# Blocks 0 and 1 of a two-network kernel run as one pair of half blocks

## The chip, the cores and the metric

The kernel runs on one core of a Trainium2 chip. Five engines matter: PE multiplies matrices, DVE (vector) and ACT (scalar) do elementwise work, POOL (GpSimd) does a few integer additions here, and SP issues nearly all transfers between HBM and the core's memory. The metric is the time of one execution in device microseconds, and less is better.

## The reference

Packed attention runs first: 32 packed queries p of each batch and head attend over k and v, and the 576 queries q then attend over the 32 packed results, which serve as keys and as values. The output is reordered to 4608 rows of 512 and goes through two networks, one with ELU and one that multiplies two products. The four large weights come as float64.

```python
def _attn_ref(q, k, v, p):                 # 8 batches, 8 heads, 576 x 64
    def sm_attn(qq, kk, vv):
        s = scale * np.matmul(qq, kk.transpose(0, 1, 3, 2))
        s = s - np.max(s, axis=-1, keepdims=True)
        a = np.exp(s)
        a = a / (np.sum(a, axis=-1, keepdims=True) + 1e-09)
        return np.matmul(a, vv)
    p_packed = sm_attn(p, k, v)            # 32 rows per head
    return sm_attn(q, p_packed, p_packed)
...
    h = x @ w_in                           # 4608x512 @ 512x2048
    g = np.where(h > 0.0, h, alpha * (np.exp(np.minimum(h, 0.0)) - 1.0))
    x = g @ w_out                          # 2048x512
...
    return (x @ w_a) * (x @ w_b) @ w_out2  # 512x1536, 1536x512
```

## The kernel before

A product in f32 is made of three matmuls: each factor is split in a high part, which ACT copies and rounds, and a low part, which DVE subtracts. So nearly every result that PE needs next passes ACT and then DVE.

**The first network** works on the batches as blocks. A block has two halves h of 288 rows and 16 slices f of the hidden width. One pair (h, f) is a step: `l1` (six matmuls, L453) multiplies the attention result `a2` of this half with packed weights `wr`; `act1` makes the ELU, with two passes on ACT (L461, L462), `gf` on DVE (L465), and the split `gr` with its high part on ACT (L467) and its low part on DVE (L469); two steps later `l2` (twelve matmuls, L475) adds gr times `wout` to four accumulators. The accumulators of a half go out through `x2_out`.

Attention is folded into the weights: `wp` multiplies 512 columns of w_in by the packed result of a batch, and `wps` splits that into one slot of a ring (`ring_r`, five slots of two tiles, L83). Four such chunks c serve the slices f = 4c to 4c+3 of both halves. The probabilities of q over the packed keys are made by `s2`, `s2t` (a transpose, L338), `sm2a` (row maximum L343, subtraction L344), `sm2b`, `sm2c` (L357, L358) and `sm2d`, which leaves them as a tile `a2` (L363, L365) for each half h and each r, four tiles in all. Ahead of that lie, for each batch, the transposes of k and q (`qkT`), `s1`, `sm1`, `aT`, `pp`, `pps` and `ppT`.

**Block 0** runs f 0 to 7 of both halves, then f 8 to 15 of both. The sums of the first part (part 1) are stored to HBM as `x2p`, and part 2 loads them and adds them on DVE (L490). Blocks 1 to 7 run all 16 slices of one half and then of the other, and need no partial sums.

**The weights of the first network** come in 32 pieces of 512 KB, 16 of w_in (`i0_0` to `i3_3`; i`c`_`j` is the j-th row block of chunk c) and 16 of w_out (`o0` to `o15`). A piece is loaded into one of five slots (tag wst) and converted from float64: two passes on ACT (L133, L134), two and one on DVE (L137, L138, L141), an integer addition on POOL (L144), and for w_out also a cast on ACT (L148) and a subtraction on DVE (L149).

**What sets the order.** Attention, conversions and loads are items with times in half steps; `run_until` emits what is due between the instructions of act1, and an item whose needs are missing waits with the rest of its chain. Up to the end of block 0 a scheduler then orders the instructions of each engine anew by its own estimate, and it may pull conversions far ahead. From block 1 on (`manual_schedule`) the order of the program is kept on PE, DVE and ACT. Each engine works its list in order, so a wait holds all that stands behind it. SP's list holds all loads and stores.

Of the kernel before, what the change touches and what calls it, by code (L numbers as in the profile page):

```python
# [20 lines left out]
P = 128  # L21
# [4 lines left out]
def program(tc, q, k, v, p, w_in, w_out, w_a, w_b, w_out2, out):  # L26
# [25 lines left out]
    RING = NCH + 1  # L52
# [8 lines left out]
    with ctx:  # L61
# [29 lines left out]
        x2p = [dram.tile([P, NDM, HS], F32, name=f"x2p{h}") for h in range(2)]  # L91
# [290 lines left out]
        def attention(b, tokens=False):  # L382

            u = []

            def add(at_half, fn, *a, takes=None, frees=None):
                u.append((at_half, lambda: fn(b, *a), takes, frees))

            def at_times(k, load_q, pt, s1s, sm1, q, sm1bs, at, at5, p, ppt, s2s, wps_):
# [92 lines left out]

        def x2_out(b, h, acc, part):

            for d0 in range(0, NDM, 2):
                t = stage.tile([P, 2, HS], F32, tag="wst", name=f"x2s{b}_{h}_{d0}_{part}")
                if part == 2:
                    nc.sync.dma_start(t, x2p[h][:, d0:d0 + 2, :])
                    for i in range(2):
                        nc.vector.tensor_tensor(t[:, i, :], acc[d0 + i][:, :HS], t[:, i, :], op=ALU.add)  # L490
                else:
                    nc.scalar.copy(t[:, 0, :], acc[d0][:, :HS])
                    nc.vector.tensor_copy(t[:, 1, :], acc[d0 + 1][:, :HS])
                nc.sync.dma_start((x2p[h] if part == 1 else x2d[b][h])[:, d0:d0 + 2, :], t)
# [84 lines left out]
        load_v(0)  # L579
        for t, fn, takes, frees in attention(0, tokens=True):  # L580
            if t > 64:
                t += 16
            elif 39 < t < 50:
                t += 27
# [342 lines left out]
```

## Time and profile before

| | us |
|---|---|
| median of three runs (1646.26 to 1648.41) | 1646.31 |
| the profiled run | 1646.58 |
| its span in the trace | 1644.8 |
| PE busy | 1569.8 |
| DVE busy | 1025.1 |
| ACT busy | 717.0 |
| POOL busy | 168.8 |

The span is what the trace covers, and 1.8 us of the profiled run lie around it. Busy shares of the whole span hide stages that differ: PE's 95% is made of a start in which it often waits and of a long rest in which it hardly does. So the rows further down are read by stretch. In them a wait names the instruction that ended it last.

### The profile page before, as it was taken

The page shows a single profiled execution, that of the slowest core. Times are in us where ns is not written, and L with a number is a line of the kernel's source. Part 1 is how long each engine was busy: PE and PEld are TensorE (multiplying, and loading weights), DVE is VectorE, ACT ScalarE, POOL GpSimd, SP SyncE. Part 2 cuts the span into 40 slices and gives each one's busy share as a digit, 9 for nine tenths or more (in the row PEclk, how much of TensorE's full clock was granted, in tenths as well). Part 3 has the DMA queues.
Part 4 walks back from the last instruction along what each step waited for, and adds up shares of the span by engine and source line. Part 5 has one row for each costly group of instructions (what it writes and reads, how often), then busy time and mean ns, then how long its engine had stood idle before and what let it go on. Part 6 is the DMA issues. An engine that isn't in the chain of part 4 may idle for free.

```text
span 1644.8 us, 27465 instructions
## 1 busy us (share of the span) xinstructions
PE 1569.8 (95%) x10824; PEld 1438.4 (87%) x10824; DVE 1025.1 (62%) x2054; ACT 717.0 (44%) x1579; POOL 168.8 (10%) x122
## 2 busy tenths in 40 slices
PE   5488999999999999999889999999999999999999
PEld 3376998989898999999788899989989989998997
DVE  6988676777777676755588735634545453563452
ACT  6675666666666666665433312312222221231211
POOL 3321010000000100011364100000000000000000
PEclk7599999999999999999999999999999999999999
DMA  8755334525262624114366745535445554552541
GB/s 253 179 162 129 105 102 103 131 53 142 76 158 69 154 80 110 47 66 144 117 229 233 268 148 185 221 136 207 180 166 188 213 201 147 184 208 107 211 180 39
DMA packets 214785, 247.95 MB, mean 151 GB/s; under 512 B 150144, under 2 KB 180864, under 8 KB 205440
## 3 DMA queue, kind: packets, MB, share of 16 engines
q1 hardware_dynamic: 214656, 246.19, 46.3%
q8 instruction: 85, 1.39, 0.3%
q14 instruction: 44, 0.36, 0.1%
HBM read 194.64 MB, written 51.51 MB: 150 GB/s over the span
## 4 chain that ended last, share of the span: by engine, by line
PE 79%; DVE 6%; issue 4%; ACT 3%; DMA 3%; POOL 3%; SPq 2%; DVEq 0%; POOLq 0%; ACTq 0%
PE x2a L475 21%; PE o L846 17%; PE B L802 12%; PE h L453 10%; PE C L802 8%; PE A L802 8%; POOL e L708 2%; SPq L164 1%; POOL wo L791 1%; DMA wst_i<-in_moe_w_in_dram 1%; DVE gr L469 1%; DVE gf L465 1%; PE pp L301 1%; ACT gr L467 0%; DVE wr L83 0%
## 5 line engine op out<-in xcount | busy, mean ns | idle before, releaser
L475 PE MATMUL x2a<-gr,wout 128*128 128x288 f32 x3072 | 466.2, 300 | 10.3 <-DVE gr L469 6.4
L475 PEld LDWEIGHTS x2a<-gr,wout 128*128 128x128 f32 x3072 | 424.1, 190 | 51.6 <-issue 12.3
L846 PE MATMUL o<-wo,c 128*128 128x512 f32 x1296 | 309.2, 393 | 0.0
L846 PEld LDWEIGHTS o<-wo,c 128*128 128x128 f32 x1296 | 243.7, 189 | 48.2
L802 PE MATMUL B<-s,e 128*128 128x384 f32 x1296 | 262.8, 337 | 11.1 <-DVE u L827 5.3
L453 PE MATMUL h<-a,wr 128*128 128x288 f32 x1536 | 251.2, 299 | 16.9 <-DVE gf L465 8.6
L453 PEld LDWEIGHTS h<-a,wr 128*128 128x128 f32 x1536 | 220.8, 191 | 26.4 <-DVE gf L465 12.9
L802 PEld LDWEIGHTS B<-s,e 128*128 128x128 f32 x1296 | 228.2, 189 | 15.2 <-DVE u L827 7.8
L802 PE MATMUL A<-s,e 128*128 128x384 f32 x864 | 174.7, 336 | 1.0 <-ACT p L825 1.0
L802 PE MATMUL C<-s,e 128*128 128x384 f32 x864 | 173.9, 335 | 0.0
L465 DVE SCALAR_TENSOR_TENSOR gf<-ge,h 128x288 f32<-128x288 f32 x256 | 113.7, 445 | 85.8 <-ACT ge L462 83.1
L467 ACT CAST gr<-gf 128x288 fp32r<-128x288 f32 x256 | 110.4, 432 | 129.8 <-DVE gf L465 128.7
L802 PEld LDWEIGHTS A<-s,e 128*128 128x128 f32 x864 | 153.8, 188 | 7.2 <-ACT p L825 1.3
L469 DVE TENSOR_TENSOR gr<-gf,gr 128x288 fp32r<-128x288 f32 x256 | 131.5, 514 | 34.4 <-ACT gr L467 32.3
L802 PEld LDWEIGHTS C<-s,e 128*128 128x128 f32 x864 | 152.8, 189 | 0.0
L82 ACT CAST c<-u 128x384 fp32r<-128x384 f32 x72 | 36.8, 512 | 230.3 <-DVE u L835 230.3
L461 ACT ACTIVATE ge<-h 128x288 f32<-128x288 f32 x256 | 104.5, 409 | 74.0 <-PE h L453 73.3
L832 DVE TENSOR_TENSOR v<-p,B 128x384 f32<-128x384 f32 x72 | 39.8, 552 | 143.3 <-PE B L802 143.2
L462 ACT ACTIVATE ge<-ge 128x288 f32<-128x288 f32 x256 | 113.8, 445 | 7.6
L827 DVE TENSOR_TENSOR u<-p,B 128x384 f32<-128x384 f32 x72 | 39.7, 552 | 105.1 <-PE B L802 105.1
L825 ACT COPY p<-A 128x384 f32<-128x384 f32 x72 | 34.7, 482 | 120.2 <-PE A L802 120.1
L829 ACT COPY p<-C 128x384 f32<-128x384 f32 x72 | 34.7, 482 | 102.2 <-PE C L802 102.2
(342 smaller groups left out, 1449.1 us busy)
## 6 DMA issues: line engine op xcount, KB each, us to landing
e<-ed SPq DMA_DIRECT2D x60, 1792.0 KB, 7.1
ed<-e SPq DMA_DIRECT2D x12, 1792.0 KB, 6.4
x2d<-x2s SPq DMA_DIRECT2D x32, 288.0 KB, 2.4
out_dram<-osb SPq DMA_DIRECT2D x36, 256.0 KB, 2.0
v<-in_v_dram SPq DMA_DIRECT2D x8, 1024.0 KB, 7.8
wst_i<-in_moe_w_in_dram SPq DMA_DIRECT2D x16, 512.0 KB, 5.4
wst_o<-in_moe_w_out_dram SPq DMA_DIRECT2D x16, 512.0 KB, 4.5
kst<-in_k_dram SPq DMA_DIRECT2D x112, 72.0 KB, 2.5
```

The costliest lines, as they stand in the source:

```text
L82: nc.scalar.copy(hi, src)
L453: nc.tensor.matmul(t[:, :HS], w[:, wi, o * P:(o + 1) * P], x[:, xi, :], start=(n == 0), stop=(n == 5))
L461: nc.scalar.activation(e, t[:, :HS], AF.Relu, scale=-1.0)
L462: nc.scalar.activation(e, e, AF.Exp, scale=-1.0)
L465: nc.vector.scalar_tensor_tensor(g, e, -1.0, t[:, :HS], op0=ALU.add, op1=ALU.max)
L467: nc.scalar.copy(gr[:, 0, :], g)
L469: nc.vector.tensor_tensor(gr[:, 1, :], g, gr[:, 0, :].bitcast(F32), op=ALU.subtract)
L475: nc.tensor.matmul(acc[d][:, :HS], wout_r[f][:, wi, d * P:(d + 1) * P], gr[:, xi, :], start=(first and n == 0), stop=(last and n == 2),)
L802: nc.tensor.matmul(bank[:, :HT], es[f][:, E_OF[i], wi, k * P:(k + 1) * P], ss[i][:, xi, k, :], start=(first and n == 0), stop=(n == 5), sk ...
L827: nc.vector.tensor_tensor(u, p1, pB, op=ALU.add)
L832: nc.vector.tensor_tensor(v, p1, pB, op=ALU.add)
L846: nc.tensor.matmul(acc, cr[:, xi, t * P:(t + 1) * P], wo[f][:, wi, :], start=(f == 0 and n == 0), stop=(f == NF2 - 1 and n == 2),)
```

## The change

Batches 0 and 1 run as one: part 1 is f 0 to 7 of batch 0 (both halves) and of batch 1 (both halves), part 2 is f 8 to 15 of the same four. So 32 steps run on the first eight slices and 32 on the last eight, and block 1 too stores partial sums and adds them. All eight `a2` tiles of the pair are kept. The ring has four slots: batch 0 uses slots 0 and 1, batch 1 slots 2 and 3, each twice, and from batch 2 on chunk c has slot c. The load of `x2p` is issued four steps before its adds. The first load of v stands behind the first three pieces of w_in on SP. The attention times of batches 0 and 1 are new, those of batches 2 to 7 shift a little, and o0 and o1 are converted ahead of the pieces of chunk 1. The scheduler still orders the first 32 steps; from part 2 on the program's order is kept. The new line numbers are L460 for l1, L472 for gf, L474 and L476 for gr, L482 for l2, L507 for the copy into x2s and L508 for its store.

```diff
-    RING = NCH + 1
+    RING = NCH
...
-        x2p = [dram.tile([P, NDM, HS], F32, name=f"x2p{h}") for h in range(2)]
+        x2p = [[dram.tile([P, NDM, HS], F32, name=f"x2p{b}_{h}") for h in range(2)] for b in range(2)]
...
-            a2 = m1.tile([P, 2, HS], F32R, tag="a2", name=f"a2_{b}_{h}_{r}", bufs=4)
+            a2 = m1.tile([P, 2, HS], F32R, tag="a2", name=f"a2_{b}_{h}_{r}", bufs=8)
...
-            slot = (b * NCH + c) % RING
+            slot = c if b > 1 else 2 * b + c % 2
...
-                at_times((-17, -14, -2, -1), (-13, 0), 0, (4, 6), (8, 9), (10, 11, 13, 14), 12, 14, 16, (18, 20, 21), 22, (
+                at_times((-17, -14, -4, -3), (-13, -2), -4, (4, 6), (8, 9), (10, 11, 13, 14), 12, 14, 16, (18, 20, 21), 22, (
...
-                ), (48, 52, 56, 60))
+                ), 70, (48, 52, 57, 62))
...
+        def x2_load(b, h):
+            for d0 in range(0, NDM, 2):
+                x2s[d0] = stage.tile([P, 2, HS], F32, tag="wst", name=f"x2s{b}_{h}_{d0}_2")
+                nc.sync.dma_start(x2s[d0], x2p[b][h][:, d0:d0 + 2, :])
...
-        load_v(0)
...
+        put(HEAD + 8.25, load_v, 0)
...
-        order = [("i", 0, j) for j in range(NJ)]
...
+        order = [("i", 0, j) for j in range(NJ)] + [("o", f, 0) for f in range(2)]
+        order += [("i", 1, j) for j in range(NJ)] + [("o", f, 0) for f in range(2, NF // 2)]
+        order += [("i", c, j) for c in (2, 3) for j in range(NJ)] + [("o", f, 0) for f in range(NF // 2, NF)]
...
-                t = 12 + 2.5 * (n - 16)
+                t = 8 + 2.6 * (n - 16)
...
+        def m1_steps(t0, bs, fs, part=0):
+
+            for n, (b, h, f) in enumerate([(b, h, f) for b in bs for h in range(2) for f in fs]):
+                first, last = f == fs[0], f == fs[-1]
...
+                if part == 2 and f == fs[-4]:
+                    x2_load(b, h)
...
-        m1_block(0)
+        m1_steps(0, range(2), range(NF // 2), 1)
...
-        for b in range(1, B - 1):
+        m1_steps(4 * NF, range(2), range(NF // 2, NF), 2)
+        for b in range(2, B - 1):
             m1_block(b)
```

In the lists below a row names the line, the operation, and out<-in by the program's names; the number behind a name counts tiles.

ACT at the start, before. `kT0` is the transposed k of batch 0, `win` with `wst_i0_0` the first piece of w_in, `e0` the scores of the packed queries.

```order
L209 COPY kT0_178<-kTp0_00_179 128x4x128
L209 COPY kT0_178<-kTp0_10_206 128x4x128
L133 ACTIVATE win_163<-wst_i0_0_253 128x512
L134 ACTIVATE wst_i0_0_253<-wst_i0_0_253 128x512
L133 ACTIVATE win_163<-wst_i0_1_255 128x512
L134 ACTIVATE wst_i0_1_255<-wst_i0_1_255 128x512
L257 COPY e0_0_237<-s1_0_0__239 128x288
L257 COPY e0_1_238<-s1_0_0__239 128x288
```

The same place in the changed kernel, where `wm_o0` is the first piece of w_out.

```order
L209 COPY kT0_175<-kTp0_00_176 128x4x128
L133 ACTIVATE win_163<-wst_i0_0_250 128x512
L134 ACTIVATE wst_i0_0_250<-wst_i0_0_250 128x512
L133 ACTIVATE win_163<-wst_i0_1_252 128x512
L134 ACTIVATE wst_i0_1_252<-wst_i0_1_252 128x512
L133 ACTIVATE win_163<-wst_i0_2_254 128x512
L134 ACTIVATE wst_i0_2_254<-wst_i0_2_254 128x512
L209 COPY kT0_175<-kTp0_10_203 128x4x128
L257 COPY e0_0_234<-s1_0_0__236 128x288
L257 COPY e0_1_235<-s1_0_0__236 128x288
L133 ACTIVATE wm_o0_462<-wst_o0_259 128x512
```

Three pieces of w_in have moved ahead of the second copy of kT, which stood right behind the first.

SP around the loads of o8 and o9, before. `v1` is v of batch 1, `pn2` and `kst2` are p and k of batch 2, and `x2p` the partial sums of the first half.

```order
L100 DMA pn2_1292<-in_p_dram 32x2x64 x4
L176 DMA v1_1000<-in_v_dram 128x8x256
L179 DMA v1_1000<-in_v_dram 64x8x64
L116 DMA wst_o8_1083<-in_moe_w_out_dram 128x512
L494 DMA x2p0_161<-x2s0_0_0_1_1020 128x576
L116 DMA wst_o9_1125<-in_moe_w_out_dram 128x512
L494 DMA x2p0_161<-x2s0_0_2_1_1024 128x576
L116 DMA wst_o10_1182<-in_moe_w_out_dram 128x512
L116 DMA wst_o11_1258<-in_moe_w_out_dram 128x512
```

The same place in the changed kernel.

```order
L116 DMA wst_o8_1042<-in_moe_w_out_dram 128x512
L100 DMA pn2_1127<-in_p_dram 32x2x64 x2
L176 DMA v1_925<-in_v_dram 128x8x256
L179 DMA v1_925<-in_v_dram 64x8x64
L164 DMA kst2_0_1132<-in_k_dram 32x18x32 x5
L508 DMA x2p0_0_159<-x2s0_0_0_1_1104 128x576
L164 DMA kst2_0_1132<-in_k_dram 32x18x32
L508 DMA x2p0_0_159<-x2s0_0_2_1_1108 128x576
L164 DMA kst2_0_1132<-in_k_dram 32x18x32 x2
L116 DMA wst_o9_1156<-in_moe_w_out_dram 128x512
L116 DMA wst_o10_1212<-in_moe_w_out_dram 128x512
L116 DMA wst_o11_1276<-in_moe_w_out_dram 128x512
```

The load of o8 has moved ahead of v1, and that of o9 behind v1, eight loads of kst2 and both stores of the first half's sums, where it stood behind one of these stores.

DVE at the end of the first 16 steps, before. `gr0_1_7` is step 15 and `gf0_0_8` step 16, `wr` a packed weight, `t1` the scores of batch 1.

```order
L469 TENSOR_TENSOR gr0_1_7_1290<-gf0_1_7_1288,gr0_1_7_1290 128x288
L83 TENSOR_TENSOR wr2_0_103<-wp0_2__1317,wr2_0_103 128x512
L149 TENSOR_TENSOR wout13_96<-wm_o13_1658,wout13_96 128x512
L493 COPY x2s0_1_0_1_1435<-x2a0_1_0_1_1052 128x288
L83 TENSOR_TENSOR wr2_1_104<-wp0_2__1317,wr2_1_104 128x512
L493 COPY x2s0_1_2_1_1439<-x2a0_1_0_3_1054 128x288
L465 SCALAR_TENSOR_TENSOR gf0_0_8_1382<-ge0_0_8_1362,h0_0_8_1342 128x288
L137 TENSOR_SCALAR wm_o14_1704<-wm_o14_1704 128x512
L338 STREAM_TRANSPOSE t1_1369<-s2_1_0__1370 128x288 x2
L138 TENSOR_SCALAR wm_o14_1704<-wm_o14_1704 128x512
L465 SCALAR_TENSOR_TENSOR gf0_0_9_1414<-ge0_0_9_1406,h0_0_9_1399 128x288
```

In the changed kernel step 16 is `gf1_0_0`, the first slice of batch 1, and `a2_1_0` its first factor; gr of step 15 stands 16 rows ahead of this piece.

```order
L358 STREAM_TRANSPOSE t1_1197<-t1_1197 128x288
L83 TENSOR_TENSOR wr3_0_105<-wp1_1__1415,wr3_0_105 128x512
L137 TENSOR_SCALAR wm_o15_1750<-wm_o15_1750 128x512
L365 TENSOR_TENSOR a2_1_0_0_1375<-t1_1197,a2_1_0_0_1375 128x288
L365 TENSOR_TENSOR a2_1_0_1_1386<-t1_1197,a2_1_0_1_1386 128x288
L138 TENSOR_SCALAR wm_o15_1750<-wm_o15_1750 128x512
L83 TENSOR_TENSOR wr3_1_106<-wp1_1__1415,wr3_1_106 128x512
L141 SCALAR_TENSOR_TENSOR wm_o15_1750<-wst_o15_1523,wm_o15_1750 128x512
L472 SCALAR_TENSOR_TENSOR gf1_0_0_1427<-ge1_0_0_1409,h1_0_0_1402 128x288
L149 TENSOR_TENSOR wout15_98<-wm_o15_1750,wout15_98 128x512
L472 SCALAR_TENSOR_TENSOR gf1_0_1_1469<-ge1_0_1_1459,h1_0_1_1452 128x288
L476 TENSOR_TENSOR gr1_0_0_1429<-gf1_0_0_1427,gr1_0_0_1429 128x288
```

The two subtractions of a2 and the last two conversions now stand between step 15 and step 16, where copies, the split of a packed weight and one conversion stood.

## Rows read from the trace of the kernel before

**Rows 1.** PE's busy tenths in 40 equal slices of the span (page).

```profile
PE   5488999999999999999889999999999999999999
```

**Rows 2.** Busy us by stretch: PE, PEld, DVE, ACT, POOL, clock, DMA share, GB/s.

```profile
115.00:153.00 38.00, 29.14 (x306) 21.65 (x304) 35.18 (x73) 22.60 (x53) 8.38 (x6) 1.00 0.52 136
153.00:795.00 642.00, 637.12 (x5579) 587.56 (x5580) 447.58 (x1027) 417.73 (x993) 56.48 (x42) 1.00 0.37 100
```

**Rows 3.** PE's waits, 50 to 153 us: total us, times, longest us.

```profile
PE h L453 <- DVE gf L465: 8.6, 4, 4.6
PE h L453 <- ACT a L363: 6.0, 1, 6.0
```

**Rows 4.** Timeline of PE: start us, us, instructions, idle before and its releaser.

```profile
152.92 2.24 PE L453 MATMUL h<-a,wr 128*128 128x288 f32 x12 [2.51 <-DVE gf L465]
```

**Rows 5.** Chain of work that ended last, in order of time: start us, us.

```profile
184.74 0.80 PE h L453 x6
185.54 1.59 PE x2a L475 x12
```

**Rows 6.** DVE's groups by form, 0 to 160 us: busy us, mean ns, idle before.

```profile
L469 DVE TENSOR_TENSOR gr<-gf,gr 128x288 fp32r<-128x288 f32 x24 | 13.1, 548 | 0.6 <-ACT gr L467 0.5
L465 DVE SCALAR_TENSOR_TENSOR gf<-ge,h 128x288 f32<-128x288 f32 x24 | 10.5, 444 | 2.7 <-ACT ge L462 2.7
L365 DVE TENSOR_TENSOR a<-t,a 128x288 fp32r<-128x288 f32 x6 | 3.5, 588 | 0.0
L343 DVE TENSOR_REDUCE mx<-t 128x9 f32<-128x288 f32 x8 | 3.2, 433 | 0.0
L83 DVE TENSOR_TENSOR wr<-wp__1797,wr 128x512 fp32r<-128x512 f32 x2 | 1.4, 678 | 0.0
```

**Rows 7.** Timeline of DVE, at 17 to 23 and 143 to 155 us.

```profile
17.67 1.40 DVE L138 TENSOR_SCALAR win<-win 128x512 uint32<-128x512 uint32 x1
22.75 1.40 DVE L264 TENSOR_REDUCE nm<-e 128x1 f32<-128x576 f32 x2
143.55 0.44 DVE L465 SCALAR_TENSOR_TENSOR gf<-ge,h 128x288 f32<-128x288 f32 x1
143.91 1.20 DVE L469 TENSOR_TENSOR gr<-gf,gr 128x288 fp32r<-128x288 f32 x1
154.49 0.81 DVE L469 TENSOR_TENSOR gr<-gf,gr 128x288 fp32r<-128x288 f32 x2
```

**Rows 8.** Busy us by stretch, columns as in rows 2, around the first piece.

```profile
10.00:20.00 10.00, 6.84 (x74) 3.00 (x70) 6.80 (x11) 6.07 (x11) 1.42 (x2) 0.88 1.06 353
```

**Rows 9.** Timeline of ACT, first piece of w_in and last copy of aT.

```profile
14.98 0.67 ACT L133 ACTIVATE win<-wst_i 128x512 f32<-128x512 f32 x1 [0.54 <-DMA wst_i<-in_moe_w_in_dram]
35.74 0.42 ACT L290 COPY aT<-aT5p 64x256 f32<-64x256 f32 x1
```

**Rows 10.** Timeline of DVE: the gaps at 100 to 108 us and near 133 us.

```profile
100.89 0.15 DVE L271 TENSOR_SCALAR nm<-nm 128x1 f32<-128x1 f32 x1 [0.41 <-ACT e L266]
107.72 0.43 DVE L137 TENSOR_SCALAR wm_o<-wm_o 128x512 f32<-128x512 f32 x1 [1.21 <-ACT wm_o L133]
133.75 0.46 DVE L465 SCALAR_TENSOR_TENSOR gf<-ge,h 128x288 f32<-128x288 f32 x1 [1.37 <-ACT ge L462]
```

**Rows 11.** Timeline of SP's queue: issue of o8 and of seven loads of k.

```profile
100.30 0.57 SPq L116 DMA_DIRECT2D wst_o<-in_moe_w_out_dram  x1
121.51 3.56 SPq L164 DMA_DIRECT2D kst<-in_k_dram  x7
```

**Rows 12.** DMA issues (page): count, KB each, us from issue to landing.

```profile
wst_o<-in_moe_w_out_dram SPq DMA_DIRECT2D x16, 512.0 KB, 4.5
```

**Rows 13.** Timeline of POOL: the first addition of a conversion.

```profile
17.44 1.34 POOL L144 TENSOR_TENSOR win<-win,wst_i 128x512 int32<-128x512 int32 x1 [16.14 <-DVE win L141]
```

**Rows 14.** Busy us by stretch, columns as in rows 2, around 65 us.

```profile
60.00:70.00 10.00, 6.47 (x42) 2.98 (x42) 10.00 (x21) 4.95 (x10) 2.31 (x2) 0.56 0.43 140
```

**Rows 15.** Timeline of PE behind a long wait, at 73 us.

```profile
73.35 3.25 PE L453 MATMUL h<-a,wr 128*128 128x288 f32 x12 [4.60 <-DVE gf L465]
```

More of the change, by code (lines that the diff above doesn't have):

```diff
@@ L491, in x2_out @@
                 else:
+                    t = stage.tile([P, 2, HS], F32, tag="wst", name=f"x2s{b}_{h}_{d0}_{part}")
                     nc.scalar.copy(t[:, 0, :], acc[d0][:, :HS])
                     nc.vector.tensor_copy(t[:, 1, :], acc[d0 + 1][:, :HS])
-                nc.sync.dma_start((x2p[h] if part == 1 else x2d[b][h])[:, d0:d0 + 2, :], t)
+                nc.sync.dma_start((x2p if part == 1 else x2d)[b][h][:, d0:d0 + 2, :], t)
         pend = []
@@ L578, in program @@
         load_qk_tokens(0, "k", 1)
-        load_v(0)
[L580 to L584, printed above, removed]
-            elif 50 <= t < 54:
-                t -= 12
-            elif t >= 54:
-                c = (54, 57, 60).index(t - (t - 54) % 3) + 1
-                t = 64 + (-1, 7, 31, 39)[c] + (t - 54) % 3
-            needs = [f"i{takes[2]}_{j}" for j in range(NJ)] if takes and takes != 1 and takes[0] == "wp" else ()
-            put(HEAD + t, fn, chain=0, takes=takes, frees=frees, needs=needs)
-        order = [("i", 0, j) for j in range(NJ)]
-        for g in range(2):
-            f0 = g * NF // 2
-            for f in range(f0, f0 + NF // 2):
-                if f == f0:
-                    order += [("i", c, j) for c in ((1,), (2, 3))[g] for j in range(NJ)]
-                order.append(("o", f, 0))
+        put(HEAD + 8.25, load_v, 0)
+        for b in range(B):
+            for t, fn, takes, frees, late in attention(b):
+                needs = [f"i{takes[2]}_{j}" for j in range(NJ)] if takes and takes != 1 and takes[0] == "wp" else ()
+                put(t, fn, chain=(b, late), takes=takes, frees=frees, needs=needs)
+        order = [("i", 0, j) for j in range(NJ)] + [("o", f, 0) for f in range(2)]
+        order += [("i", 1, j) for j in range(NJ)] + [("o", f, 0) for f in range(2, NF // 2)]
+        order += [("i", c, j) for c in (2, 3) for j in range(NJ)] + [("o", f, 0) for f in range(NF // 2, NF)]
         convs = []
@@ L612, in program, with m1_block @@
         conveyor(convs, [(stage, 2), (at, 1), (stage, 2)], 4)
-        for b in range(1, B):
-            for t, fn, takes, frees in attention(b):
-                late = t > 64
-                if b == 1:
-                    t = t + 2.3 if late else max(48 + t - 33, 49) if 32 < t < 36 else 14 + 0.78 * max(t, 0)
-                put(2 * NF * 2 * (b - 1) + t, fn, chain=(b, late), takes=takes, frees=frees)
-        def m1_block(b):
-            half = NF // 2 if b == 0 else NF
-            order = [(h, f) for f0 in range(0, NF, half) for h in range(2) for f in range(f0, f0 + half)]
-            for s, (h, f) in enumerate(order):
-                first, last = f % half == 0, f % half == half - 1
+        def m1_steps(t0, bs, fs, part=0):
+            for n, (b, h, f) in enumerate([(b, h, f) for b in bs for h in range(2) for f in fs]):
+                first, last = f == fs[0], f == fs[-1]
                 if first:
                     acc = []
-                t0 = 4 * NF * b + 2 * s
+                if part == 2 and f == fs[-4]:
+                    x2_load(b, h)
                 t = l1(b, h, f)
-                gr = act1(t, f"{b}_{h}_{f}", lambda n: run_until(t0 + n))
-                pend.append((b, h, f, gr, acc, first, last, f // half + 1 if half < NF else 0))
+                gr = act1(t, f"{b}_{h}_{f}", lambda i: run_until(t0 + 2 * n + i))
+                pend.append((b, h, f, gr, acc, first, last, part))
                 if len(pend) > 2:
                     run_pend()
+        def m1_block(b):
+            m1_steps(4 * NF * b, [b], range(NF))
         w2src = []
```

33 lines of the change are left out of this document (20 added, 13 removed).

## The prediction

> **What bounds the kernel now.** Read the 40 slices of PE first [rows 1]: after the first four, which show four to eight tenths, only two are under nine. Then the busy time by stretch [rows 2]: from 153 to 795 us, where the first network runs, PE works 637.1 of 642 us; from 115 to 153 us it works 29.1 of 38 us and DVE 35.2. PE's waits agree: from 50 to 153 us the two longest sums are for gf and a2, products of DVE's and ACT's lists [rows 3]. So the kernel has two parts: a head in which DVE is the bound, and from PE's last long wait (2.5 us, ended at 152.92 [rows 4]) a part that PE bounds and in which a change of order moves nothing. What the change is worth is read at one place: **when PE stops waiting, and how much PE work is then left.**
>
> A step is l1 (six matmuls, 0.80 us), act1 on ACT and DVE, and two steps later l2 (twelve matmuls, 1.59 us) [rows 5]; I number the 64 steps of blocks 0 and 1 from 0. In the kernel before, at 152.92 us, PE issues l1 of steps 22 and 23 and then l2 of step 20 [rows 4].
>
> **What is left for PE.** In the changed lists PE stops waiting at l2 of step 17, which needs that step's gr: until then a2 of batch 1 (two subtractions on DVE) holds l1 of steps 16 and 17, as the lists of the change show. At that point l1 of step 19 has been done. Against the old handover that leaves two more l1 and three more l2, 2 x 0.80 + 3 x 1.59 = 6.4 us. Three wp are left in both (wp1_1, wp1_2, wp1_3 then; wp0_3, wp1_2, wp1_3 now). So the time changes by (H - 152.9) + 6.4 us, H being the end of gr of step 17 in the changed kernel. It breaks even at H = 146.5 us.
>
> **DVE's work up to H.** Counted in the lists, DVE's instructions up to that gr are those it had before up to gr of step 21 (the second of a pair that ends at 155.3 us [rows 7]), less 4 gf, 4 gr, 2 row maxima, 2 subtractions of them and 1 wr, plus 2 of a2. By the groups [rows 6], a subtraction of a maximum taken at gf's 0.44, that is 1.78 + 2.19 + 0.87 + 0.89 + 0.68 - 1.18 = 5.2 us; one instruction starts some 0.08 us before the record of the last ends (143.55 + 0.44 against 143.91 [rows 7]), so 4.5 us. All sixteen w_out conversions stay ahead of step 17 although f 8 to 15 are not wanted before step 32: the scheduler fills DVE with them early. With the waits of before, H = 155.3 - 4.5 = 150.8 us, already 4.3 us too late to break even.
>
> **DVE's waits.** Four terms.
> The start. v (1,152 KB) no longer stands ahead of the first w_in piece, which ACT waited for until 14.98 us, while the transfers ran at 353 GB/s [rows 8, 9]: 3.4 us of transfer, so the piece comes at about 11.5 us. But ACT's list now holds three pieces (six instructions, 3.4 us, and two more landings of 1.5 us) ahead of its second copy of kT, which came before them, and DVE's second copy of kT moves behind two pieces. The row maximum stays at about 23 us instead of 22.75 [rows 7], and later two casts of wout (each like the 0.67 us at 14.98) stand before the copies of qT and aT, so the last copy of aT moves from 35.74 to about 39 us [rows 9]; pp, pps and the first s2t follow at about +1 us. I take +1.0; from -3 (the lead carries, less 0.4) to +2.
> The gap after step 7. Before, DVE waited five times between 100 and 108 us, 3.4 us together, the first 0.41, the last 1.21 us for piece o8 [rows 10]. Now o8 is converted earlier and o9 has to end the gap; in SP's list its load stands behind v1, eight kst2 and both x2p stores, and these wait for l2 of step 7. From gr of step 5 PE needs 3 x 1.59 + 2 x 0.80 + 1.0 (aT) = 7.4 us to there; the five issues on SP up to o9 take 2 us more (0.5 us for one of kst [rows 11]), the landing 4.5 us [rows 12], ACT 0.7 us: 14.6 us, in which DVE has 8.0 us of work. A gap of 6.6 us for 3.4: +3; from 0 (the load is early) to +5.5 (o8 took 7.4 us from its issue at 100.30 to DVE at 107.72 [rows 10, 11], 2.2 more than 4.5 + 0.7).
> The two gaps at 129 to 134 us, 2.6 us with the second of 1.37 [rows 10], have their like at wout15, which waits for POOL's add and ACT's cast: 1.8 us for 2.6, -0.8.
> POOL's adds. A DVE instruction that falls into one ends late: 1.40 us, to 19.07 us, for what takes 0.43 at 107.72, with the add from 17.44 to 18.78 us [rows 7, 10, 13]; the last such is the gr of 1.20 us. In 25 of the 32 adds of the conversions I count such a stretch, 22.8 us together. Going by what stands behind each add in the changed list I count some 18; part of that goes to ACT's turn at the start, so -1.0; from -4 to +1.
> [...]
>
> H = 150.8 + 1.0 + 3.0 - 0.8 - 1.0 = 153.0 us. After it DVE still finishes batch 1, and PE waits some 0.3 us more. The change is 153.0 - 152.9 + 6.4 + 0.3 = **+6.8 us**. The profiled run took 1646.58 us (span 1644.8), 0.27 above the median of 1646.31; the forecast is 1653.1 us beside the median.
>
> **Edits at nothing.** Block 1 now also goes over HBM: eight x2p stores and eight loads for four and four, and eight more adds of some 0.45 us (gf has their size [rows 6]) on DVE, 3.6 us spread over 110 us in which DVE idles three tenths [rows 2]; the loads are issued four steps (9.6 us) ahead. Uncovered, the accumulator's banks would hold PE at the ends of the halves, 0 to 2 us in all. The ring of four: the wr of chunk 3 is written after l1 of step 31, for which ACT waits anyway, and wanted twelve steps later: 0. Eight a2 tiles take no time. The earlier k transposes and pT of batches 2 to 7 move inside covered time: -0.5 to +0.5 us.
>
> **Rivals.**
> No change: the first piece's lead is kept (-3 instead of +1) and o9's load is not late (0 instead of +3). H = 146.0 and the time 1646.1 us; with one of the two, 1649.1 to 1650.1. For it speaks that DVE is at 10.00 of 10 us from 60 to 70 us [rows 14], so that a lead on DVE carries unless ACT or a transfer breaks it; against it, ACT's list.
> [...]
> [...]
> [...]
>
> **How the numbers follow.** The forecast (1650 to 1654.5) has 0.56, the clock on top of it (to 1658) 0.13, no change 0.20, faster 0.11. Within 0.2% means 3.3 us here, about what a measurement of this kernel tells from no change. Slower 0.69, same 0.20, faster 0.11. The range takes in no change in its middle (about 1646) and the clock: 1646 to 1658, leaving out what is faster and the ends.
>
> **What would show it.** In the profile after: the first w_in piece on ACT near 11.5 us; the second copy of kT on DVE near 18 us; s2t of the first half near 48 us; a DVE gap of 6 us ended by a w_out piece near 115 us; PE's last long wait for a2 or gf ending near 144 us and gr of step 17 near 153.0 us; from there PE without gaps. Wrong would make it a DVE that has finished all w_out pieces before 140 us, or PE working through from 135 us.

## The result and the profile after

The changed kernel takes 1659.87 us (1658.72 to 1662.27) beside 1646.28 us for the kernel before on the same chip: a ratio of 1.0083, with a 95% interval of 1.0066 to 1.0101. It is slower by 13.6 us. Slower was forecast, but by 6.8 us, and 1659.87 lies outside the range of 1646 to 1658. The profiled run took 1659.0 us with a span of 1657.2, 12.4 us above the span before. Executions that the chip ran far slower (1709 to 7798 us) are left out of all times below; the profiled run of e6 was one of them (3089.6 us), so no trace of e6 is read.

Two lines of the stretches of the changed kernel, columns as in [rows 2], of which they are the counterpart:

```profile
115.00:153.00 38.00, 28.50 (x263) 22.23 (x255) 33.72 (x70) 24.71 (x54) 10.14 (x7) 0.91 0.38 122
153.00:795.00 642.00, 629.72 (x5559) 581.83 (x5551) 445.71 (x1029) 412.31 (x981) 56.48 (x42) 1.00 0.39 107
```

The head looks as before: 28.5 us of PE in 38 where there were 29.1. The surprise is the second line. There PE had 637.1 us of work in 642 [rows 2], and now has 629.7: 7.4 us were lost in the part in which the prediction said that PE would work without gaps. PE's waits from 170 to 800 us name them (us in total, times, longest), 12.7 us together, where the same stretch before has 4.4:

```profile
PE pTp L107 <- issue: 6.1, 5, 1.4
PE x2a L482 <- DVE x2s L503: 3.3, 3, 2.2
PE x2a L482 <- ACT x2s L506: 1.5, 2, 1.0
PE h L460 <- DVE gf L472: 0.6, 1, 0.6
```

Two smaller lines are left out, aT5p for aT (0.7 us, before 0.6) and l2 for gr (0.5, before 2.1).

The sum can be laid along the steps. The table gives the start of l1 of a step in the timeline of PE (each step is the same amount of l1 work in both kernels):

| l1 of step | before | after | later by |
|---|---|---|---|
| 32 | 182.03 | 185.52 | 3.5 |
| 72 | 293.32 | 304.19 | 10.9 |
| 224 | 713.54 | 726.47 | 12.9 |
| end of span | 1644.8 | 1657.2 | 12.4 |

At step 32 PE still has two wp of batch 1 to do that were done by then in the kernel before, 2 x 1.09 us. So the head costs 3.5 + 2.2 = 5.7 us in this run, steps 32 to 72 another 10.9 - 3.5 - 2.2 = 5.2, steps 72 to 224 another 2.1, and the rest gives 0.5 back.

**The signs in the head** came as written. Lines of the timelines of ACT and DVE of the changed kernel:

```profile
11.65 0.66 ACT L133 ACTIVATE win<-wst_i 128x512 f32<-128x512 f32 x1 [1.61 <-DMA wst_i<-in_moe_w_in_dram]
37.47 0.45 ACT L290 COPY aT<-aT5p 64x256 f32<-64x256 f32 x1
18.64 1.06 DVE L209 COPY kT<-kTp 128x512 f32<-128x512 f32 x1 [0.79 <-PE kTp L200]
47.33 0.84 DVE L338 STREAM_TRANSPOSE t<-s__446 128x288 f32<-128x288 f32 x2
117.42 0.43 DVE L137 TENSOR_SCALAR wm_o<-wm_o 128x512 f32<-128x512 f32 x1 [3.33 <-ACT wm_o L133]
153.79 0.41 DVE L476 TENSOR_TENSOR gr<-gf,gr 128x288 fp32r<-128x288 f32 x1
```

The first piece comes 3.3 us earlier than in [rows 9], and the last copy of aT 1.7 us later all the same. DVE's gap after step 7 ends with the piece o9; with the eight smaller ones from 105 us on it comes to 7.8 us for the 3.4 of [rows 10]. gr of step 17 ends at 154.20 us, 1.2 us behind the forecast of 153.0. PE's last waits before it, 3.00 and 0.80 us for a2 of batch 1, end at 144.98 us (forecast 144). From there PE has no wait over 0.5 us up to 205 us.

**The signs behind it** failed. Where the last l2 of a half is followed by the first of the next, and at pTp, PE stands still. First PE and then DVE of the changed kernel, around the end of batch 0's second half (steps 47 to 50):

```profile
242.02 1.83 PE L482 MATMUL x2a<-gr,wout 128*128 128x288 f32 x12 [2.22 <-DVE x2s L503]
```

```profile
240.67 0.46 DVE L365 TENSOR_TENSOR a<-t,a 128x288 fp32r<-128x288 f32 x1 [0.83 <-ACT a L363]
241.05 0.45 DVE L476 TENSOR_TENSOR gr<-gf,gr 128x288 fp32r<-128x288 f32 x1
241.42 1.54 DVE L503 TENSOR_TENSOR x2s<-x2a,x2s 128x288 f32<-128x288 f32 x4
```

The four adds that free the accumulators stand in DVE's list behind a subtraction of attention, which waits for ACT, and behind gr of the step; they take 1.54 us in a row, and PE's next l2 starts 0.15 us after the first of them ends (241.42 + 0.45 = 241.87 us). PE had finished the half's last l2 by 238.4 us, so the adds were held for 3 us by what stands ahead of them in the list.

And around the pTp of batch 4; those of batches 3 and 5 to 7 look alike (PE, then DVE, of the changed kernel; then the same place before):

```profile
366.19 0.30 PE L107 MATMUL pTp<-ident,pn 128*128 128x128 f32 x1 [1.18 <-issue]
```

```profile
365.40 0.69 DVE L83 TENSOR_TENSOR wr<-wp__4413,wr 128x512 fp32r<-128x512 f32 x1 [0.65 <-ACT wr L82]
```

```profile
360.44 0.30 PE L107 MATMUL pTp<-ident,pn 128*128 128x128 f32 x1 [0.19 <-PE h L453]
```

The profile says "issue", that is, it shows no releaser. DVE's line does: the split of wp2's second tile ends at 365.40 + 0.69 = 366.09 us, and pTp, which takes the same pair of banks, starts 0.10 us later. Before, pTp waited 0.19 us.

### The profile page after: what moved, and what is told of

Read it like the earlier page. It is cut to its first block, busy times and chain, and to the rows that moved or that the text cites. A ratio compares the mean times of both kernels' runs of the same rounds, so it can differ in the third digit from the quotient of the medians.

```text
span 1657.2 us, 27471 instructions
## 1 busy us (share of the span) xinstructions
PE 1571.2 (95%) x10824; PEld 1441.2 (87%) x10824; DVE 1025.2 (62%) x2062; ACT 717.5 (43%) x1579; POOL 168.9 (10%) x122
## 4 chain that ended last, share of the span: by engine, by line
PE 79%; DVE 7%; issue 4%; ACT 3%; POOL 3%; DMA 2%; SPq 1%; DVEq 0%; POOLq 0%; ACTq 0%
PE x2a L482 21%; PE o L846 17%; PE B L802 12%; PE h L460 10%; PE C L802 8%; PE A L802 8%; POOL e L708 2%; POOL wo L791 1%; DVE gf L472 1%; SPq L164 1%; DMA wst_i<-in_moe_w_in_dram 1%; DVE gr L476 1%; PE pp L301 1%; DVE wr L83 1%; DVE wm_o L137 0%
## 5 line engine op out<-in xcount | busy, mean ns | idle before, releaser
L482 PE MATMUL x2a<-gr,wout 128*128 128x288 f32 x3072 | 464.8, 300 | 16.0 <-DVE gr L476 7.6
L482 PEld LDWEIGHTS x2a<-gr,wout 128*128 128x128 f32 x3072 | 424.0, 190 | 56.7 <-ACT ge L469 13.6
L460 PE MATMUL h<-a,wr 128*128 128x288 f32 x1536 | 251.6, 299 | 21.4 <-ACT a L363 9.9
L460 PEld LDWEIGHTS h<-a,wr 128*128 128x128 f32 x1536 | 221.8, 192 | 29.8 <-DVE gf L472 13.1
L474 ACT CAST gr<-gf 128x288 fp32r<-128x288 f32 x256 | 110.5, 432 | 135.5 <-DVE gf L472 134.6
L472 DVE SCALAR_TENSOR_TENSOR gf<-ge,h 128x288 f32<-128x288 f32 x256 | 113.8, 445 | 87.4 <-ACT ge L469 85.1
L476 DVE TENSOR_TENSOR gr<-gf,gr 128x288 fp32r<-128x288 f32 x256 | 129.9, 508 | 41.3 <-ACT gr L474 39.5
```

The source lines that it names most:

```text
L460: nc.tensor.matmul(t[:, :HS], w[:, wi, o * P:(o + 1) * P], x[:, xi, :], start=(n == 0), stop=(n == 5))
L472: nc.vector.scalar_tensor_tensor(g, e, -1.0, t[:, :HS], op0=ALU.add, op1=ALU.max)
L474: nc.scalar.copy(gr[:, 0, :], g)
L476: nc.vector.tensor_tensor(gr[:, 1, :], g, gr[:, 0, :].bitcast(F32), op=ALU.subtract)
L482: nc.tensor.matmul(acc[d][:, :HS], wout_r[f][:, wi, d * P:(d + 1) * P], gr[:, xi, :], start=(first and n == 0), stop=(last and n == 2),)
```

## The experiments

All are edits of the changed kernel unless the kernel before is named; ratios are to the kernel before, with their 95% intervals. Four hold the same DVE list as the changed kernel up to step 17, and yet their l1 of step 32 starts at 185.16 (e15), 186.83 (e2b), 187.56 (e1) and 188.72 us (e2a) beside its 185.52. The differences are there by step 14; where they come from is open. So costs of one or two us are read from how the distance between two traces grows over the steps that an edit touches, and only larger ones from the medians.

### The times of batches 2 to 7

**e1_pT_back** puts pT alone back.

```diff
-                at_times((-17, -14, -4, -3), (-13, -2), -4, (4, 6),
+                at_times((-17, -14, -4, -3), (-13, -2), 0, (4, 6),
```

> One number of the changed kernel goes back: in batches 2 to 7 pT stands at half step 0 instead of -4. The changed kernel took 1659.9 us. Theory: pTp stands too close behind the split of wp2's second tile, whose banks it takes, and PE waits for that subtraction on DVE, 1.18 us where it waited 0.19 before; by the starts of the steps each block is 0.48 us longer for it, since later steps win some back. Five blocks: -2.4 us, 1657.5, and pTp waits 0.2 us again. Rival one: the whole wait counts, five times 1.0 us and more: 1654.7. Rival two: the growth per block comes from the earlier k and q, not from pT: 1659.9, and the waits go elsewhere.

It is far slower, 1673.24 us (1.0157, 1.0137 to 1.0178). All three theories had it wrong, and yet the first one's mechanism is there: at half step 64 pT stands right behind the split of wp3, which the change moved to 62, and waits for that one longer. PE of e1, from its second block of this kind:

```profile
379.18 0.30 PE L107 MATMUL pTp<-ident,pn 128*128 128x128 f32 x1 [2.16 <-issue]
379.24 2.24 PE L482 MATMUL x2a<-gr,wout 128*128 128x288 f32 x12
381.27 1.65 PE L460 MATMUL h<-a,wr 128*128 128x288 f32 x6
382.71 2.30 PE L482 MATMUL x2a<-gr,wout 128*128 128x288 f32 x12
384.85 0.96 PE L460 MATMUL h<-a,wr 128*128 128x288 f32 x6
```

and its stretch from 379 to 385 us, columns as in [rows 2]:

```profile
379.00:385.00 6.00, 5.82 (x33) 5.85 (x34) 2.01 (x6) 2.07 (x6) 0.00 (x0) 0.72 0.50 89
```

The wait is 2.16 us instead of 1.18, and behind it six matmuls of l1 take 1.65 us instead of 0.96: the granted clock of the stretch is 0.72, where the changed kernel has 1.00 around this pTp (366 to 372 us). Between steps 72 and 200 three of four blocks are 2.7 us longer than in the changed kernel, 1.0 us of wait and the rest slow matmuls. In the fourth pTp waits just as long, but the twelve matmuls of l2 behind it take 1.86 us instead of 2.24, and the block is 1.1 us longer. Its l2 behind pTp:

```profile
470.92 0.30 PE L107 MATMUL pTp<-ident,pn 128*128 128x128 f32 x1 [2.16 <-issue]
470.97 1.86 PE L482 MATMUL x2a<-gr,wout 128*128 128x288 f32 x12
```

So the wait goes with the distance from the last wp to pT: 0.19 us at four half steps (before), 1.18 at three (changed), 2.16 at two (e1).

**e6_wp56** moves wp2 half a step ahead instead.

```diff
-                ), 70, (48, 52, 57, 62))
+                ), 70, (48, 52, 56, 62))
```

> One number of the changed kernel: in batches 2 to 7 wp2 stands at half step 56 instead of 57, so that pT at 60 comes one step's half later behind its split. Theory: pTp waits for DVE's subtraction of wp2's second tile; the five waits of 1.2 to 1.4 us fall below 0.3 us, each block gets 0.5 us shorter: 1657.5. Rival: the split itself waits for the ring's slot, which l1 of the block's step 27 frees, so that it comes no earlier: 1659.9 and the waits as they were.

1654.8 us (1.0049, 1.0031 to 1.0066): 5.1 us faster than the changed kernel, what rival one of e1 would give. That it is pTp is shown by the kernels with this edit and others below: from step 72 to 224, which the other edits don't touch, e8 takes 418.2 us and e15 418.3, the changed kernel 422.3. In e8 each of the four blocks with a pTp there is 1.0 to 1.1 us shorter, nearly the whole wait of 1.18.

**e10_times** gives the kernel before these times and nothing else of the change.

```diff
-                at_times((-17, -14, -2, -1), (-13, 0), 0, (4, 6),
+                new = b > 1
+                at_times((-17, -14, -4, -3) if new else (-17, -14, -2, -1), (-13, -2) if new else (-13, 0), -4 if new else 0, (4, 6),
...
-                ), (48, 52, 56, 60))
+                ) , (48, 52, 57, 62) if new else (48, 52, 56, 60))
```

> The kernel before with another part alone: the times of k, q, pT and wp of batches 2 to 7 as in the changed kernel, ring and blocks as before. Theory: pTp waits 1.2 us for the split of wp2 in batches 3 to 7, each block gets 0.5 us longer: 1647 + 2.5 = 1649.5. Rival: with five slots in the ring the splits come earlier and the times cost nothing: 1647.

1652.22 us (1.0033, 1.0020 to 1.0046): 5.1 us slower, twice what was expected. PE's waits in it, from 155 to 815 us:

```profile
PE pTp L107 <- issue: 5.9, 5, 1.2
```

From step 32 to 224 its trace takes 536.1 us where the kernel before takes 531.5, 4.6 us more. So the times cost alone what the prediction put at nothing.

### The accumulators of part 2

**e2b_early** puts the end of a half, in part 2, ahead of act1 of the step whose l1 has been issued.

```diff
                 t = l1(b, h, f)
+                if part == 2 and len(pend) == 2 and pend[0][6]:
+                    run_pend()
                 gr = act1(t, f"{b}_{h}_{f}", lambda i: run_until(t0 + 2 * n + i))
```

> In part 2 alone, at the end of a half, the last l2 of the half with its adds is put ahead of act1 of the step whose l1 has just been issued, so that DVE's four adds no longer stand behind that step's gf, gr and attention. Theory: the three waits of PE for x2s (2.22, 0.56, 0.50 us, 3.3 together) come from DVE's list order, the banks being free for the adds long before; they fall to 0.3 us in all and the kernel to 1656.9. Rival: the 1.5 us that gf and gr then come later hold l2 two steps on, and the time stays at 1659.9.

**e2a_noadd** leaves the addition out; two copies on ACT and two on DVE take its place.

```diff
                 if part == 2:
                     t = x2s[d0]
-                    for i in range(2):
-                        nc.vector.tensor_tensor(t[:, i, :], acc[d0 + i][:, :HS], t[:, i, :], op=ALU.add)
+                    nc.scalar.copy(t[:, 0, :], acc[d0][:, :HS])
+                    nc.vector.tensor_copy(t[:, 1, :], acc[d0 + 1][:, :HS])
```

> The addition of the stored partial sums is left out (they are loaded all the same); the four accumulators of a half go out by two copies on ACT and two on DVE, as in part 1. Theory: the waits for x2s are the four adds in a row on DVE (1.54 us) and what stands ahead of them; with half of it on ACT the 2.22 falls to some 1.4 us and the other two to 0: -1.9 us, 1658.0. Rival: the load of the partial sums is what is late; then the waits stay at 3.3 us, since the tile is still waited for, and the time at 1659.9.

By their medians, 1659.95 (1.0075, 1.0060 to 1.0090) and 1657.35 us (1.0061, 1.0046 to 1.0076), they say little. By the steps e2b takes 2.1 us from the changed kernel between steps 46 and 60, and e2a 2.2 us between 46 and 72. At the place above, first e2b and then e2a:

```profile
241.25 1.82 PE L482 MATMUL x2a<-gr,wout 128*128 128x288 f32 x12 [0.16 <-DVE x2s L503]
```

```profile
244.21 1.99 PE L482 MATMUL x2a<-gr,wout 128*128 128x288 f32 x12 [1.21 <-ACT x2s L502]
```

2.22 us become 0.16 with the adds moved up, and 1.21, ended by ACT, with the adds replaced. It is the place of the adds in DVE's list, not the load of the partial sums, which e2b has too. What e2b won it lost again at step 62: there its pTp of batch 3 waits 1.89 us instead of 1.41, and l1 behind it takes 1.64 us where the changed kernel has 0.96.

**e3_sched** lets the scheduler order part 2.

```diff
         m1_steps(0, range(2), range(NF // 2), 1)
+        m1_steps(4 * NF, range(2), range(NF // 2, NF), 2)
         ET = mybir.EngineType
...
         in_order.add("all")
-        m1_steps(4 * NF, range(2), range(NF // 2, NF), 2)
```

> The scheduler orders part 2 too, and the program's order is kept only from step 64 on. Theory: the waits of PE for x2s at the ends of the halves of part 2 (3.3 us) come from the program's order, in which the four adds stand behind gf, gr and attention; ordered by the scheduler, as part 2 of block 0 was before, they fall to 0.8 us and the time to 1657.4. Rival: the scheduler moves later work of block 2 forward and other waits take their place, 1660 to 1663.

1661.30 us (1.0088, 1.0073 to 1.0103). The waits for x2s do fall, to 1.4 us, but others take their place (from 170 to 815 us gr 3.5 us where the changed kernel has 1.7, gf 1.4 for 0.6). The distance to the changed kernel goes from 1.3 us at step 24 up to 8.2 and is 2.4 from step 64 on. The rival holds.

### DVE's list in the head

**e4_o_late** converts o11 to o15 from step 32 on.

```diff
-                t = 8 + 2.6 * (n - 16)
+                t = 8 + 2.6 * (n - 16) if n < 27 else 64 + 2.3 * (n - 27)
...
-                if n == 2:
+                if n == 2 and i + NSTAGE < 27:
                     load(i + NSTAGE)
...
-            for i in range(NSTAGE):
-                put(convs[0][0] - NLEAD + i * 0.1, load, i)
+            for i in (*range(NSTAGE), *range(27, len(convs))):
+                put(convs[0][0] - NLEAD + i * 0.1 if i < 27 else convs[i][0] - 9, load, i)
...
-            put(times[0] - 16, w2_load, i)
+            put(times[0] - (16 if i > 5 else 5), w2_load, i)
```

> The pieces o11 to o15 are loaded and converted from step 32 on, one each 1.15 steps, and not in the first 32 steps (the first six loads of the second network's words are issued 11 half steps later, for the slots). Theory: the head is DVE's list: up to gr of step 17 it loses five conversions of some 2.2 us and two of their stretches by POOL, 12 us together, so that gr comes at 142 us instead of 154.2; afterwards DVE has 3 us of work in a step of 2.4 us from step 32 to 38, which gives 4 us back: 1652. Rival one: transfers or ACT bound the head, gr of step 17 stays near 152 us: 1660 to 1664. Rival two: everything moved is given back at steps 32 to 38: 1660.

**e5_o_mid** converts them at steps 21 to 29, and keeps the program's order from step 16 on. The first two edits to the loads are those of e4.

```diff
-                t = 8 + 2.6 * (n - 16)
+                t = 8 + 2.6 * (n - 16) if n < 27 else 42 + 4 * (n - 27)
...
-        m1_steps(0, range(2), range(NF // 2), 1)
+        m1_steps(0, [0], range(NF // 2), 1)
...
         in_order.add("all")
+        m1_steps(2 * NF, [1], range(NF // 2), 1)
```

> The pieces o11 to o15 are converted at half steps 42, 46, 50, 54 and 58 (steps 21 to 29) and loaded nine half steps ahead of that; so that no scheduler pulls them forward, the program's order is kept from step 16 on instead of from step 32. Theory: the head is DVE's list, and these five conversions are 11 us of it, as e4_o_late showed; placed where DVE has half of its time free (13.9 of 30 us busy from 170 to 200 us) nothing is given back: PE's last wait for a2 ends near 134 us, and the time is 1649 (to 1653 if the program's order makes PE wait between steps 16 and 32). Rival: the program's order from step 16 costs as much as is gained, by waits for attention's results: 1660.

1666.04 (1.0115, 1.0100 to 1.0130) and 1665.72 us (1.0112, 1.0095 to 1.0129). The head is DVE's list: l1 of step 16 starts at 134.92 us in e4 and at 131.99 in e5 instead of 143.65, though e4 was 2.6 us late at step 12. But nothing of it is left. In e4 l1 of step 48 is 7.9 us later than in the changed kernel, in e5 l1 of step 32 is 5.0 us later. PE of e4, around l1 of steps 38 and 39:

```profile
203.32 2.69 PE L482 MATMUL x2a<-gr,wout 128*128 128x288 f32 x11 [3.27 <-DVE gr L476]
208.72 1.81 PE L460 MATMUL h<-a,wr 128*128 128x288 f32 x6 [2.71 <-DVE gf L472]
```

and a stretch of it, columns as in [rows 2]:

```profile
198.00:216.00 18.00, 11.36 (x54) 10.05 (x52) 12.82 (x27) 9.66 (x22) 2.57 (x2) 0.72 0.21 64
```

DVE is busy 12.8 of 18 us and PE starves all the same: in program order DVE waits for ACT's casts (2.34 us before one split of a packed weight), PE waits for DVE, and its granted clock is 0.72 on average. The free half of DVE's time from 170 to 200 us, on which e5's expectation rested, was not to be had in these two lists.

**e11_no_add** leaves out POOL's additions.

```diff
-                nc.gpsimd.tensor_tensor(m.bitcast(I32), m.bitcast(I32), low.bitcast(I32), op=ALU.add)
+                if store is not None:
+                    nc.gpsimd.tensor_tensor(m.bitcast(I32), m.bitcast(I32), low.bitcast(I32), op=ALU.add)
```

> The changed kernel with POOL's 32 integer additions of the first network's conversions left out (a part of the conversion; ACT's and DVE's passes stay). Theory: up to gr of step 17 DVE is stretched by them 22 times, 21 us in all, and DVE's list is the head: gr of step 17 comes some 18 us earlier and the time falls to 1642. Rival: the head is held by ACT, by transfers and by attention's chain, and the stretch fills time that DVE would wait in anyway: 1652 to 1656.

1651.27 us (1.0026, 1.0011 to 1.0041): 8.6 us faster than the changed kernel, between the two. At step 16 it is 11.1 us ahead of the changed kernel, at step 32 8.2 us. So of the 21.1 us of stretch (22 DVE instructions that end late in an add; before, counted in the same way, 25 with 23.6 us, for which the prediction has 22.8) under half reaches the end; from 115 to 153 us PE works only 26.3 of 38 us there, and waits for a2 and for ACT's part of gr. The edit also made the scheduler order DVE's list anew (260 instructions ahead of the last gr of the first 18 steps instead of 255), so the 8.6 us are not the additions alone.

### The first load of v

**e7_v_first** puts it back in front.

```diff
-        put(HEAD + 8.25, load_v, 0)
+        load_v(0)
```

> The first load of v goes back in front of the pieces of w_in, all else as changed. Theory: the place of v gave DVE's list no lead, since ACT's list took it (the last copy of aT came at 37.5 us, 1.7 us later than before): the time falls by some 1 us or stays, 1659, and s2t of the first half starts no later. Rival: the piece that came at 11.65 us instead of 14.98 is a lead that carries to the end, 3 us: 1663.

1656.43 us (1.0056, 1.0041 to 1.0071): 3.4 us faster than the changed kernel, and l1 of step 32 starts at 181.56 us instead of 185.52. **e9_v_behind** makes the opposite edit in the kernel before (`put(HEAD + 8.25, load_v, 0)` for `load_v(0)`).

> The kernel before with one part of the change alone: the first load of v stands behind the first three pieces of w_in. Theory: as in the changed kernel, ACT turns to the pieces before its second copy of kT, all of the attention of batch 0 comes later and nothing is won on DVE: 1647 + 3 = 1650. Rival: there the lead of the piece carries, and the cost seen in e7 belongs to the changed order of the conversions: 1644 to 1647.

1645.48 us (0.9990, 0.9979 to 1.0001): no cost, if anything a gain of 1.7 us. The same edit costs in one order and not in the other. **e14_conv** tries the order of the conversions.

```diff
-        order = [("i", 0, j) for j in range(NJ)] + [("o", f, 0) for f in range(2)]
-        order += [("i", 1, j) for j in range(NJ)] + [("o", f, 0) for f in range(2, NF // 2)]
+        order = [("i", c, j) for c in range(2) for j in range(NJ)] + [("o", f, 0) for f in range(NF // 2)]
```

> The changed kernel with the conversions of the first half in the old order: all of chunk 1 ahead of o0 and o1, v behind the first pieces as changed. Theory: v's place costs 3.4 us in the changed kernel (e7) and nothing in the kernel before (e9), and what differs there is that o0 and o1 are loaded and converted right behind v and ahead of chunk 1, so that chunk 1, for which wp1 at step 2 waits, comes later: 1656.4. Rival: the order of these pieces is not it: 1660.

1657.85 us (1.0069, 1.0055 to 1.0083): 2.0 us, some of it. The lists show what differs: ahead of gr of step 4 DVE has 24 conversions in the changed kernel, 23 in e14 as in the kernel before and in e9, and 21 in e7. The scheduler answers to the place of a load with another number of conversions pulled ahead of the first steps. That fits the order of the medians (1659.87, 1657.85 and 1656.43 us for 24, 23 and 21 in the changed order), but no run sets this number alone, so it isn't shown as the cause. pps, the end of batch 0's chain, starts at 42.5 us in the changed kernel and in e7, so the chain of attention is not what v's place moves.

### Together

**e8_three** has v first, wp2 at 56 and the adds ahead (e7, e6, e2b); **e15_two** the last two alone; **e16_four** all of e8 and the old order of e14. The diffs are those above.

> Three edits of the changed kernel at once: v first (e7), wp2 at half step 56 (e6), and in part 2 the adds of a half's end ahead of act1 (e2b). Theory: they are three separate costs of the change, 3.4 us in the head (e7 against the changed kernel), 3.1 us of pTp's waits in batches 3 to 7 (e6), and 2 to 3 us of waits for the accumulators: 1659.9 - 9 = 1651, still 4 us above the kernel before, which is what is left for PE at the handover less DVE's shorter list. Rival: they overlap, because a wait that goes in one place leaves PE earlier at the next: 1655 to 1656.

> The changed kernel with wp2 at half step 56 and the adds of a half's end ahead of act1, v behind the pieces as changed: e8 without its v edit. Theory: v's place is worth 3.4 us in the changed order: 1652. Rival: e7's lead was a run of another landing order, and e8's 1648.6 comes from the other two edits alone: 1649.

> The changed kernel with four edits: v first, wp2 at half step 56, the adds of a half's end ahead of act1 (as e8), and the old order of the first conversions, chunk 1 ahead of o0 and o1 (e14 took 2.0 us from the changed kernel with it). Theory: the paired blocks and eight a2 tiles, freed of the change's other parts, cost nothing any more: 1646.6, the kernel before within 0.1%. Rival: v first has taken what the order of the conversions gave, and 1648.6 stays.

| kernel | us | ratio to before | interval |
|---|---|---|---|
| changed | 1659.87 | 1.0083 | 1.0066 to 1.0101 |
| e15_two | 1653.06 | 1.0040 | 1.0026 to 1.0054 |
| e8_three | 1648.57 | 1.0004 | 0.9992 to 1.0017 |
| e16_four | 1651.67 | 1.0032 | 1.0019 to 1.0044 |

Two edits behind the head take 6.8 us, and v first another 4.5. Taken singly they gave 5.1 (e6), 3.4 (e7) and some 2 us (e2b by the steps), 10.5 for e8's 11.3, so they hardly overlap; e8 stands where the kernel before stands. By the steps, e15 is 6.0 us shorter than the changed kernel from 32 to 224; of the lead in e8's own trace 2.7 us arise behind step 224, where none of its edits acts and where e7 and e15 show 0.3, so a few us of that lead belong to the one run. PE's waits in e8 from 153 to 815 us, the first four lines:

```profile
PE x2a L482 <- DVE gr L476: 2.1, 6, 0.8
PE pTp L107 <- issue: 1.1, 1, 1.1
PE x2a L482 <- DVE x2s L503: 0.7, 2, 0.6
PE aT5p L289 <- ACT aT L283: 0.6, 1, 0.6
```

The 6.1 us of pTp have become 1.1 (the one in part 2 is left) and the 3.3 us for x2s 0.7. e16 is 3.1 us slower than e8: the old order of conversions, which won 2 us beside v behind, loses beside v first. Its list has 23 conversions ahead of gr of step 4 again where e8, like e7, has 21. With e15, whose list has 24, the medians go with this number again (1653.06, 1651.67, 1648.57). The two gains don't add up, and the rival holds.

**e12_before56** and **e13_before56_v** bring the better times to the kernel before (as e10 with 56 for 57; e13 with e9's edit too).

> The kernel before with the changed times of k, q and pT in batches 2 to 7 and wp2 at half step 56, wp3 at 62. Theory: pT's cost and gain are one distance, that from the split of wp2 or wp3 to pTp; with wp2 at 57 the wait cost 1.0 us a block (e8 lost it all), and with wp2 at 56 and pT ahead of wp3 PE neither waits for the split nor loses the 0.5 us that it lost at pTp before (e8 gained 0.57 us a block on the kernel before from step 72 to 224). On the old blocks that is 5 times 0.57: 1647.2 - 2.9 = 1644.3. Rival: the gain is one of the ring of four or of the paired blocks; then 1647.

> As e12_before56, with the first load of v behind the first three pieces of w_in too (e9 alone: 1645.5 against 1647.2). Theory: the two lie in different stages and add up: 1642.6. Rival: the 1.7 us of e9 were not there, since steps 32 to 72 of its trace stood only 0.2 us earlier: 1644.3.

1647.21 (1.0002, 0.9993 to 1.0011) and 1645.62 us (0.9992, 0.9984 to 1.0001). In e12 pTp no longer waits, but no block gets shorter, since the wait has moved one step on. PE of e12:

```profile
356.81 1.09 PE L240 MATMUL wp__4492<-win,ppT 64*32 64x512 f32 x16 [0.47 <-DVE pT L109]
```

wp3 now waits for DVE to copy pT out of the banks that both use. e8's gain on the kernel before, 0.5 to 0.6 us in each of the blocks from step 72 to 200, doesn't come with the times alone; what of it belongs to the other lists stays open. No version here is clearly faster than the kernel before: e9 and e13 are 0.1% below it, with intervals that touch 1.

## Why the prediction was wrong

**The head came out near its sum, in part by luck.** Forecast +6.8, measured +5.7 in this run, and by the same rule (l1 of step 32, plus the two wp) 5.3, 7.0, 7.7 and 8.9 in the four kernels with the same list. DVE was the bound, as said (e4, e5), but single terms were off and made up for each other.
- DVE's work and the gaps: H was forecast at 153.0 and came at 154.2 us. The late load of o9 took the gap that was worked out for it; the lists gave 21.1 us of stretch by POOL for 23.6, a gain of 2.5 us for the -1.0 that was taken. (The 4.5 us of less work come to 4.4 by the prediction's own numbers, eleven instructions at 0.08 us, which changes nothing.)
- What is left for PE: 154.2 would give +8.0 by the formula. The trace has 5.7, and two things make up the difference. The kernel before lost time behind its own handover: from 152.92 to 182.03 us its granted clock was 0.94 on average and in the changed kernel, from 153.32 to 185.52, 1.00; 0.06 of 29.1 us is 1.7 us, an estimate. Its twelve matmuls in 2.24 us stand in [rows 4], and the prediction's sum doesn't book them. And four of the twelve matmuls of l2 of step 17 started from 153.32 us on, ahead of the end of gr, 0.5 us that was not left any more.
- The start, +1.0, was too small. e7 and e8 against e15 put 3.4 to 4.5 us on v's place, and the working that gave +1.0 (ACT's turn delays attention) is not how it acts: attention's chain ended at the same time, and the list of DVE changed.
- So a start 2.4 to 3.5 us too small stood against 1.7 us of clock and 1.5 us of POOL's stretch the other way.

**The step that failed is "Edits at nothing".** Two of its sentences.
- "The earlier k transposes and pT of batches 2 to 7 move inside covered time: -0.5 to +0.5 us." They cost 5.1 us in the kernel before (e10), and in the changed kernel one number gets 5.1 us back (e6). The cover that was meant is DVE's and ACT's idle time; but PE executes pTp in its list, and pTp takes the banks that wp2 has just filled. The wait before it, 0.19 us, could be seen in the trace of before, as could the distance that made it short: wp3 at 60 and pT at 64. The change made the distance three half steps, 57 to 60, and PE waits 1.2 us.
- "Uncovered, the accumulator's banks would hold PE at the ends of the halves, 0 to 2 us in all." The mechanism was named, and 0 was taken. It was 3.3 us by the waits, 2.1 of it to be had back (e2a, e2b). The loads were covered, as said; the adds were not, since from step 32 on the program's order puts them behind gr and behind attention, where the scheduler had put the adds of block 0 early enough that PE had no wait for them.
Together with the 0.6 us for gf these are the 5.2 us of steps 32 to 72 (3.3 + 0.6 + one pTp, 1.4 for 0.2 before). The other four pTp cost 4 us more than before, of which steps 72 to 224 show 2.1; about 0.5 us a block comes back elsewhere, as in e8, and what gives it back is open.

**The rivals.** No change and faster were wrong. Less stretch by POOL's additions did come (21.1 us for 23.6), but e11 shows that even none of it would leave the changed kernel at 1651. The 0.13 for the clock and the end of the range at 1658 hold a term whose size no run shows. The traces show in its place a granted clock of 0.91 from 115 to 153 us after 1.00 before [rows 2]: ten matmuls of l1 of steps 16 and 17 took 2.34 us from 144.98 us on, at 0.61 from there to 147.40 us, and DVE waited 0.97 us for ACT's part of step 16 behind them. No run separates what that cost; H was only 1.2 us late in all.

## What to carry over

Moving an instruction in the list of the engine that is the bound has to be priced, even where the other engines are idle: look up which banks or buffers it takes, who reads them last, and how many steps lie between, and take the wait that the trace shows there now as the start of the sum. An order that is kept as written puts a result that frees a resource behind everything written ahead of it; at the ends of accumulations write the emptying first. And where a scheduler orders a part, an edit to a load can come back as another order of another engine, so compare the lists before pricing the edit itself.

## What was unexpected in the hardware

In these traces a wait of PE of about 2.2 us cost itself or nearly twice itself. After 2.22 us at 242.02 us in the changed kernel twelve matmuls took 1.83 us, at a clock of 1.00 from 242 to 246 us; in e1 the same wait, 2.23 us, was followed by 3.22 us for twelve, at 0.58 from 244 to 248 us, and 2.16 us at 379.18 by six matmuls in 1.65 us, at 0.72 from 379 to 385 us. The waits at e1's five pTp are alike (10.8 us together, the longest 2.2), and yet behind the one at 287.25 us the twelve matmuls of l2 took 2.36 us, behind the one at 379.18 us 2.24 and behind the one at 470.92 us 1.86. Behind the changed kernel's five waits at pTp, one of 1.41 and four of 1.18 us, they took 1.86 to 1.87 us, each in a stretch of 6 us with a clock of 1.00.
